# A fused attention and two-layer MLP kernel: its first stage in fixed instruction sequences, with three pairs' row sums made behind the values product

## The chip, the cores and the metric

One core of a Trainium2 chip runs the whole program. The metric is device time in microseconds, median of the runs; lower is better. The before kernel has 880.47 us.

## What is computed

The reference is windowed attention, its output laid out as 2304 tokens of 512 columns, then two MLP layers, all in f32:

```python
scores = scale * np.matmul(q, k.transpose(0, 1, 3, 2))      # 4 batches, 8 heads, 576 positions, 64 columns
mask = (rel >= 0) & (rel < 64)                              # rel = query position - key position
scores = np.where(mask, scores, -1000000000.0)
attn = np.exp(scores - np.max(scores, axis=-1, keepdims=True))
attn = attn / (np.sum(attn, axis=-1, keepdims=True) + 1e-09)
x = np.matmul(attn, v)                                      # then (2304, 512)
x = np.maximum(x @ w_in, 0.0) ** 2 @ w_out                  # 512 -> 2048 -> 512
x = (x @ w_a) * (x @ w_b) @ w_out2                          # 512 -> 1536 -> 512
```

## The kernel before

**Two stages.** In the first, attention runs together with the first six of sixteen blocks of 128 hidden columns of the first layer (`G1`). In the second (`paired`, from the first `ps_in` product at L1062 to the end) the other ten and the second layer run in a form that saves products. The change rewrites the first stage; the second keeps its code.

**Attention** goes by 18 pairs `c` of 64-query chunks (128 tokens). One pair is this chain of steps, each a key that the code names: loads `k`, `q`, `v`; `S` (scores of eight heads in two groups `j`, TensorE, L375); `M` (mask, scale and row minimum, DVE, L392); `E` (exponential with its row sums in an accumulator, ACT, L403); `N` (1 over the sum, times the probabilities, DVE, L410 to L417); `Tr` (transpose, TensorE, L437); `pT` (copy out of PSUM, ACT, L441); `V` (product with the values, which gives the output transposed, TensorE, L451); `xh`, `xl` (the output split in a high and a low half, ACT L460 and DVE L464).

**The first layer** goes by units `k`: one block of hidden columns for a block of tokens (`BLOCKS`; for the first 512 tokens in halves of 256). `H` is the projection, three products for each of four parts (high times high, high times low, low times high), `r` the relu, `g` and `hi` squares, `lo` the difference, `O` the product with `w_out` into four PSUM banks. In the first token block `H.k.0` and `O.k.0` are the two products that need only high halves. Weights are loaded as 64-bit floats (`ld`) and split on ACT and DVE (`high`, `low`, `sign`, `shift`, `sum`, then `whi`, `wlo`). After the last block `ev` and `st` move the sums to DRAM.

**What sets the order.** Every step is put in a `Plan` with its engine, an assumed cost, what it depends on and a rank; `Plan.issue` lays the steps out by a greedy list schedule and records the instructions in that order, and each engine then runs its own queue strictly in order. `PHASE` gives the ranks. In its first 45 us the plan also places fillers: where it expects TensorE to be free, `busy` (L419) records products with a bf16 identity that nobody reads, at L431 into the next step's own bank, at L424 into an old one. The SP queue issues nearly all loads and stores; `k` of pair 0 goes on ACT's queue.

Of the kernel before, what the change touches and what calls it, by code (L numbers as in the profile page):

```python
# [38 lines left out]
    "i0 o0 p0 p1 i1 p2 o1 p3 a0 i2 a1 o2 p4 b2 a2 b0 p5 i3 o3 i4 a3 b1 f4 o4 b3 i5 f5 n n p6 p7 n n p8 p9 n n p10 "  # L39
    "n n p11 x0 p12 n n n p13 n n n p14 p15 x1 x2 n p16 o5 p17 n n n n n n n n n"  # L40
# [4 lines left out]
FORM = "vvaavaaavavvvavaaaaavvvvvvaaaaaavaaavavvavvvaaavvaaaaavavvvvvava"  # L45
LATER = 4
NPR = NCH // 2
# [12 lines left out]
class Plan:  # L60
# [10 lines left out]
    def add(self, key, eng, cost, fn, deps=(), rank=0.0, take=None, give=None, size=0.0, lag=0.0):  # L71
        assert key not in self.at, key
        self.at[key] = len(self.steps)
        self.steps.append((key, eng, cost, fn, [d for d in deps if d is not None], rank, take, give, size, lag))

    def fill(self, order, slots):
# [11 lines left out]
        for t, _, i in order:  # L88
            key, eng, cost = self.steps[i][:3]
            if eng == "PE" and t < FILL_END:  # L90
                if t - at > 0.45 and (key[0] in ("S", "Tr", "V") or key[0] == "H" and len(key) == 3):
# [6 lines left out]
    def issue(self):  # L98
# [19 lines left out]
        held_to = {}  # L118

# [3 lines left out]
        while len(order) < n:  # L123
            best = None
            for eng, c in cand.items():
                opts = []
                for i in c:
# [23 lines left out]
            cand[eng].remove(i)  # L151
            if eng == "PE":
                if of_run(key) and not in_run:
                    cost += 0.23
                in_run = of_run(key)
            free[eng] = t + cost
            end = t + cost + (0.22 if eng == "PE" else 0.16)
# [21 lines left out]
def kernel(  # L179
# [51 lines left out]
    zero_bf = mk_p.tile([P, 1], BF16, name="zero_bf")  # L231

    plan = Plan({"w": 4, "ev": 3, "pr": 5})
# [59 lines left out]

    def c_hi(i):
        hi = T["wh", seq[i]] = ring_w.tile([P, 512], F32R, tag=f"wh{i}", name="wh")
        T["wl", seq[i]] = ring_w.tile([P, 512], F32R, tag=f"wl{i}", name="wl")
        nc.scalar.copy(out=hi, in_=T["a", i])
# [6 lines left out]
    cv_done, s_done = [], []  # L304

    def conv_raw(key, rank):
# [9 lines left out]
        add(("high", i), "ACT", 0.58, f(c_high), [("ld", i), *cv_free], rank)  # L316
        add(("low", i), "ACT", 0.65, f(c_low), [("ld", i), *cv_free, s_free], rank)
        add(("sign", i), "DVE", 0.35, f(c_sign), [("ld", i), *cv_free, s_free], rank)
        add(("shift", i), "DVE", 0.34, f(c_shift), [("high", i)], rank)
        add(("sum", i), "DVE", 0.61, f(c_sum), [("shift", i), ("low", i), ("sign", i)], rank)  # L320
        return i

    def conv(key, rank):
        i = conv_raw(key, rank)
        f = lambda g: (lambda: g(i))
        add(("whi", i), "ACT", 0.52, f(c_hi), [("sum", i)], rank)
        add(("wlo", i), "DVE", 0.61, f(c_lo), [("whi", i)], rank)
# [79 lines left out]

    def a_plus(c, j):
# [3 lines left out]
    def a_norm(c, j):  # L412
# [4 lines left out]
        nc.vector.tensor_tensor(out=p, in0=p, in1=ri.unsqueeze(2).to_broadcast([P, NHP, P]), op=ALU.mult)  # L417

# [54 lines left out]
    last_h = {}  # L473
# [13 lines left out]
    def attention(c, rank):  # L487
        f = lambda g, *a: (lambda: g(c, *a))
# [8 lines left out]
        for j in range(2):  # L497
            ps = ("S", c) if c >= S_ACC and j else None
            add(("M", c, j), "DVE", 0.88, f(a_max, j), [("S", c), old("Tr", j), "masks"], rank, give=ps)
            pool = c >= ON_POOL  # L500
            add(("E", c, j), "ACT", 1.57, f(a_exp, j), [("M", c, j), old("Tr", j)], rank, lag=-0.6)
            if pool:
                add(("n", c, j), "POOL", 0.4, f(a_plus, j), [("E", c, j)], rank)
            add(("N", c, j), "DVE", 0.87 if pool else 1.02, f(a_norm, j), [("n" if pool else "E", c, j)], rank)
# [8 lines left out]
            add(("pT", c, j), "ACT", 0.49, f(a_copy, j), [("Tr", c, j), old("V")], rank, give=("Tr", c, j))  # L513
        after = [("Tr", c + 1, 0)] if JOIN <= c + 1 < NPR else []
        add(("V", c), "PE", 1.08 if run else 1.1, f(a_values), [("pT", c, 0), ("pT", c, 1), ("v", c), *after], rank, take="w")
        add(("xh", c), "ACT", 0.49, f(a_xh), [("V", c), *window_free(x_of[c][0])], rank)
        add(("xl", c), "DVE", 0.61, f(a_xl), [("xh", c)], rank, give=("V", c))
# [52 lines left out]
    def unit1(t, u, cols, rank):  # L570
        k = len(units)
        n = cols.stop - cols.start
# [930 lines left out]
```

## Time and profile before

| | us |
|---|---|
| median of 3 runs (lowest, highest) | 880.47 (879.64, 881.55) |
| span of the profiled execution | 878.4 |
| TensorE busy in it | 869.8 (99%) |
| DVE, ACT busy in it | 590.1 (67%), 490.1 (56%) |

The page gives the profiled execution by its span alone; no time of its own stands beside it. Busy time is modelled from pipelined products and counts the fillers, so 99% does not say that TensorE does useful work all the time: for that one reads its waits and the fillers' rows.

### The profile page before, as it was taken

What the parts mean: (1) busy time and instruction counts of PE and PEld (TensorE: products, weight loads), DVE (VectorE), ACT (ScalarE), POOL (GpSimd) and SP (SyncE); (2) the same over time, 40 slices, a digit from 0 to 9 for tenths busy, and PEclk for the clock granted to TensorE, in tenths of its full rate; (3) what the DMA queues carried; (4) which work ended last, traced back from release to release, by engine and by line L of the source; (5) the groups of instructions that cost most, each with busy time, mean ns of one, the idle gap of its engine ahead of it and who ended that gap; (6) DMA issues with size and microseconds to landing.
All of it is one profiled execution on the core that took longest, in us unless ns stands there. A gap on an engine that the chain in (4) does not pass through costs nothing.

```text
span 878.4 us, 15421 instructions
## 1 busy us (share of the span) xinstructions
PE 869.8 (99%) x5689; PEld 804.0 (92%) x5689; DVE 590.1 (67%) x1416; ACT 490.1 (56%) x1173; POOL 12.5 (1%) x49
## 2 busy tenths in 40 slices
PE   8999999999999999999999999999999999999998
PEld 4888988888999999999999999899999999999987
DVE  6999858668774777466878747776743687343424
ACT  7998867658773667356665554655522554221301
POOL 1000000000000000000000000000000000000000
PEclk9999999999999999999999999999999999999999
DMA  9996966747898637649596797424847352636331
GB/s 325 320 323 207 363 239 207 279 178 291 287 378 329 226 125 272 253 147 385 179 397 235 268 355 297 140 91 131 293 159 259 140 182 83 242 143 215 144 132 72
DMA packets 79562, 204.03 MB, mean 232 GB/s; under 512 B 7296, under 2 KB 33152, under 8 KB 79488
## 3 DMA queue, kind: packets, MB, share of 16 engines
q1 hardware_dynamic: 78816, 202.67, 64.4%
q8 instruction: 45, 0.74, 0.4%
q10 hardware_dynamic: 672, 0.39, 0.1%
q14 instruction: 29, 0.24, 0.1%
HBM read 146.41 MB, written 56.62 MB: 231 GB/s over the span
## 4 chain that ended last, share of the span: by engine, by line
PE 95%; DMA 2%; DVE 1%; ACT 1%; issue 0%; SPq 0%
PE acc L238 13%; PE acc L239 13%; PE acc L240 13%; PE ps_aX L1062 9%; PE ps_bX L1062 9%; PE ps_inX L1062 7%; PE ps_aZ L1062 4%; PE ps_bZ L1062 4%; PE ps_inZ L1062 4%; PE ps_in L238 2%; PE ps_in L239 2%; PE ps_in L240 2%; PE ps_bY L1062 2%; PE ps_aY L1062 2%; PE ps_inY L1062 2%; PE ps_s L375 2%
## 5 line engine op out<-in xcount | busy, mean ns | idle before, releaser
L1098 ACT COPY e<-ps_aX 128x384 f32<-128x384 f32 x36 | 17.3, 481 | 98.2 <-PE ps_aX L1062 96.6
L403 ACT ACTIVATE p<-p,nm 128x128 f32<-128x128 f32 x144 | 55.8, 391 | 7.5 <-DVE nm L392 7.5
L1062 PE MATMUL ps_inX<-xb,w 128*128 128x384 f32 x270 | 54.0, 334 | 0.0
L277 ACT ACTIVATE s<-raw 128x512 uint16<-128x512 uint32 x68 | 53.4, 786 | 0.0
L272 ACT ACTIVATE a<-raw 128x512 f32<-128x512 f32 x68 | 45.5, 669 | 13.1 <-DVE w L997 5.8
L292 DVE CUSTOM_DVE_ANT_0 a<-a,s 128x1024 uint16<-128x1024 uint16 x68 | 46.4, 688 | 7.5 <-ACT s L277 6.2
L1062 PEld LDWEIGHTS ps_inX<-xb,w 128*128 128x128 f32 x270 | 47.5, 188 | 0.0
L1062 PE MATMUL ps_bX<-xb,w 128*128 128x384 f32 x234 | 46.9, 334 | 0.0
L1062 PE MATMUL ps_aX<-xb,w 128*128 128x384 f32 x210 | 42.4, 336 | 0.0
L1062 PEld LDWEIGHTS ps_bX<-xb,w 128*128 128x128 f32 x234 | 41.3, 188 | 1.0
L1102 DVE TENSOR_TENSOR e<-e,ps_aY 128x384 f32<-128x384 f32 x18 | 10.0, 554 | 46.5 <-PE ps_aY L1062 42.5
L1314 DVE TENSOR_TENSOR pr<-acc,pr 128x512 f32<-128x512 f32 x33 | 22.5, 689 | 27.5 <-PE acc L240 15.3
L1062 PEld LDWEIGHTS ps_aX<-xb,w 128*128 128x128 f32 x210 | 37.1, 188 | 1.2
L729 DVE TENSOR_TENSOR hl<-bt,hl 128x768 fp32r<-128x768 f32 x33 | 31.4, 953 | 8.7 <-ACT hl L726 8.7
L240 PE MATMUL acc<-w,gh 128*128 128x512 f32 (+1 forms) x95 | 36.8, 387 | 0.0
L239 PE MATMUL acc<-w,gh 128*128 128x512 f32 (+1 forms) x95 | 36.7, 387 | 0.0
L238 PE MATMUL acc<-w,gh 128*128 128x512 f32 (+1 forms) x95 | 36.5, 384 | 0.0
L238 PE MATMUL acc<-eh,wh 128*128 128x512 f32 (+1 forms) x96 | 36.1, 376 | 0.0
L238 PE MATMUL ps_in<-win,wh 128*128 128x512 f32 (+1 forms) x96 | 35.5, 370 | 0.0
L239 PE MATMUL acc<-el,wh 128*128 128x512 f32 (+1 forms) x96 | 34.9, 363 | 0.0
L240 PE MATMUL acc<-eh,wl 128*128 128x512 f32 (+1 forms) x96 | 34.9, 363 | 0.0
L240 PE MATMUL ps_in<-win,wl 128*128 128x512 f32 (+1 forms) x96 | 34.8, 363 | 0.0
(238 smaller groups left out, 2517.1 us busy)
## 6 DMA issues: line engine op xcount, KB each, us to landing
xb<-xop SPq DMA_DIRECT2D x44, 768.0 KB, 9.2
x<-xop SPq DMA_DIRECT2D x35, 768.0 KB, 6.6
xop<-hl SPq DMA_DIRECT2D x33, 768.0 KB, 4.8
raw<-in_w_out_dram SPq DMA_DIRECT2D x28, 512.0 KB, 4.7
q_sb<-in_qbd_dram SPq DMA_DIRECT2D x18, 512.0 KB, 6.7
pr<-part SPq DMA_DIRECT2D x48, 192.0 KB, 4.4
part<-pr SPq DMA_DIRECT2D x36, 256.0 KB, 2.5
pr<-part SPq DMA_DIRECT2D x33, 256.0 KB, 3.5
```

Source lines behind the costliest of these rows:

```text
L238: nc.tensor.matmul(ps, ah, bh, start=first, stop=False)
L239: nc.tensor.matmul(ps, ah, bl, start=False, stop=False)
L240: nc.tensor.matmul(ps, al, bh, start=False, stop=last)
L272: nc.scalar.activation(out=cv_tiles(i)[0], in_=T["raw", i][:, :, 1].bitcast(F32), func=AF.Copy, scale=2.0 ** -112)
L277: nc.scalar.activation(out=cv_tiles(i)[1][:, :, 0], in_=T["raw", i][:, :, 0], func=AF.Copy, scale=2.0 ** -29)
L292: nc.vector.tensor_tensor(out=a, in0=a, in1=s, op=ALU.add)
L375: nc.tensor.matmul(T["s", c, j][e * W:(e + 1) * W, hp, :], T["q", c][r, e, hp, r], T["k", c][r, hp, e * W:e * W + P], start=True, stop=Tru ...
L403: nc.scalar.activation(out=T["p", c, j][:, hp, :], in_=T["p", c, j][:, hp, :], func=AF.Exp, bias=T["nm", c, j][:, hp:hp + 1], scale=-1.0, ...
L729: nc.vector.tensor_tensor(out=hl(n)[:, 1], in0=view(o), in1=hl(n)[:, 0].bitcast(F32), op=ALU.subtract)
L1062: nc.tensor.matmul(ps, w[:, a, cs], x[:, b, c], start=o < 3 and not c and not n, stop=c == 1 and n == 2, skip_group_check=True,)
L1098: nc.scalar.copy(out=c_tile(i), in_=T[copied[i][0], q])
L1314: nc.vector.tensor_tensor(out=ev, in0=T["acc2", ri, s, m][f.start // 256][:, f], in1=ev, op=ALU.add)
```

## The change

Five things change, all in the first stage.

1. `SEQUENCE` lists, for TensorE, DVE, ACT and SP, the keys of the first stage in a fixed order; `Plan.issue` takes from an engine's list first and falls back to the greedy choice when it is used up. Where a key stands in a list also says on which engine the step runs (`on`, `either`), so copies, relus and `whi` may go to DVE instead of ACT.
2. Pairs 0 to 2 (`DEFER`) skip `N`. Their exponentials have no accumulator; `V` is made with operands swapped (`a_rows`: tokens in rows), and beside it eight products of the unscaled probabilities with a column pair of ones give the row sums; `R` (`a_quotient`) multiplies the result by 1 over the sums; `Tx` (`a_turn`) transposes it by four products; then `xh`, `xl`.
3. `PHASE` names unit and token block, so blocks of hidden columns come in another order.
4. `hi` may be a copy of `g` on DVE (`cut`), `r` a maximum on DVE.
5. The assumed costs are new numbers; the fillers are placed by the same rule, also before `Tx`.

```diff
+SEQUENCE = {
+    "PE": (
+        "S.0 S.1 Tr.0.0 Tr.0.1 V.0 Tr.1.0 Tx.0 Tr.1.1 S.2 V.1 Tr.2.0 Tx.1 S.3 Tr.2.1 H.0.0 H.0 V.2 Tr.3.0 O.0.0 Tx.2 "
+        "S.4 H.1.0 H.1 Tr.3.1 S.5 V.3 H.2.0 O.0 H.2 O.1.0 H.3.0 Tr.4.0 Tr.4.1 H.3 O.1 H.4.0 S.6 V.4 H.4 O.2.0 H.5.0 "
+        "O.2 H.5 O.3.0 H.6.0 O.3 H.6 O.4.0 Tr.5.0 Tr.5.1 S.7 V.5 O.4 H.7.0 O.5.0 H.7 O.5 H.8.0 O.6.0 H.8 Tr.6.0 S.8 "
...
+DEFER = "111000000000"
...
+        named = {key if isinstance(key, str) else ".".join(map(str, key)): i for key, i in self.at.items()}
+        first_of = {eng: [named[w] for w in names.split()][::-1] for eng, names in SEQUENCE.items()}
...
+                if first_of.get(eng):
+                    c = [i for i in c if i == first_of[eng][-1]]
...
+    def a_exp_only(c, j):
...
+            nc.scalar.activation(
+                out=T["p", c, j][:, hp, :], in_=T["p", c, j][:, hp, :], func=AF.Exp,
+                bias=T["nm", c, j][:, hp:hp + 1], scale=-1.0,
+                accum_out=T["rd", c][:, hp, j:j + 1] if DEFER[c] == "2" else None,
+            )
...
+    def a_rows(c):
...
+                for e in range(2):
+                    r = slice(e * W, (e + 1) * W)
+                    nc.tensor.matmul(
+                        o[r, h * D:(h + 1) * D], T["pT", c, j][:, hp, r], T["v", c][:, e, h * D:(h + 1) * D],
+                        start=True, stop=True,
+                    )
+                if DEFER[c] == "1":
+                    nc.tensor.matmul(
+                        total[:, 2 * h:2 * h + 2], T["pT", c, j][:, hp, :], ones, start=True, stop=True,
+                    )
...
+    def a_quotient(c):
...
+        nc.vector.tensor_scalar(out=ri, in0=sums, scalar1=1e-9, scalar2=None, op0=ALU.add)
+        nc.vector.reciprocal(out=ri, in_=ri)
+        nc.vector.tensor_tensor(
+            out=T["p", c, 0].rearrange("p a (b d) -> p (a b) d", d=D),
+            in0=T["o", c].rearrange("p a (b d) -> p (a b) d", d=D),
+            in1=ri.unsqueeze(2).to_broadcast([P, 2 * NHP, D]), op=ALU.mult,
+        )
+
+    def a_turn(c):
...
+        for f in range(KC):
+            nc.tensor.transpose(ps[:, f, :], T["p", c, 0][:, f, :], ident)
...
+            if cut:
+                top(T["hi", k], T["g", k])
+            else:
+                nc.scalar.activation(out=T["hi", k], in_=T["r", k], func=AF.Square)
...
+        nc.gpsimd.memset(ones, 1.0)
```

Two places show how the instructions move. The first is the start of SP's queue, which issues the loads (`raw` is a weight load, `q_sb`, `k_sb`, `v_sb` the attention inputs). Before:

```order
L269 DMA raw_152<-in_w_in_dram 128x1024
L269 DMA raw_157<-in_w_out_dram 128x1024
L348 DMA q_sb_177<-in_qbd_dram 128x2x512
L344 DMA k_sb_179<-in_kT_dram 128x4x192
L348 DMA q_sb_181<-in_qbd_dram 128x2x512
L359 DMA v_sb_183<-in_vwin_dram 64x512
L360 DMA v_sb_183<-in_vwin_dram 64x512
L356 DMA v_sb_183<-in_vwin_dram 128x512
```

And in the changed program:

```order
L434 DMA q_sb_154<-in_qbd_dram 128x2x512
L434 DMA q_sb_159<-in_qbd_dram 128x2x512
L430 DMA k_sb_179<-in_kT_dram 128x4x192
L339 DMA raw_181<-in_w_in_dram 128x1024
L445 DMA v_sb_183<-in_vwin_dram 64x512
L446 DMA v_sb_183<-in_vwin_dram 64x512
L442 DMA v_sb_183<-in_vwin_dram 128x512
L339 DMA raw_187<-in_w_out_dram 128x1024
```

The two query loads and the keys of pair 1 now stand ahead of both weight loads. The second place is TensorE around the values of pair 0, with the transposes of pair 1 behind them (`ps_p` holds transposed probabilities, `ps_o` the values product, `ident_bf` marks a filler). Before:

```order
L437 MATMUL ps_p<-ident,p 128x128 x4
L431 LDWEIGHTS ident_bf
L431 MATMUL ps_o<-ident_bf 128x512
L431 LDWEIGHTS ident_bf
L431 MATMUL ps_o<-ident_bf 128x512
L431 LDWEIGHTS ident_bf
L431 MATMUL ps_o<-ident_bf 128x512
L451 MATMUL ps_o<-pT,v_sb 64x64 x16
L437 MATMUL ps_p<-ident,p 128x128 x4
```

In the changed program, from the last of the eight products with ones to the turn (L603, into `ps_x`):

```order
L581 MATMUL ps_p<-ones,pT 128x2
L543 MATMUL ps_p<-ident,p 128x128 x4
L537 LDWEIGHTS ident_bf
L537 MATMUL ps_x<-ident_bf 128x512
L537 LDWEIGHTS ident_bf
L537 MATMUL ps_x<-ident_bf 128x512
L537 LDWEIGHTS ident_bf
L537 MATMUL ps_x<-ident_bf 128x512
L537 LDWEIGHTS ident_bf
L537 MATMUL ps_x<-ident_bf 128x512
L603 MATMUL ps_x<-ident,p 128x128 x4
```

Products with ones stand between the values products, and the turn, a step of its own, stands behind the next pair's transposes with four fillers ahead of it. In all, TensorE's queue has 55 fillers before and 25 now: 7 before `S.0`, 4 before `S.1`, 4 before `V.0`, 4 before `Tx.0` and 6 before `Tr.2.0`.

## Rows read from the trace of the kernel before

**Rows 1.** The page: TensorE's busy time, and its granted clock by slice.
```profile
PE 869.8 (99%) x5689; PEld 804.0 (92%) x5689; DVE 590.1 (67%) x1416; ACT 490.1 (56%) x1173; POOL 12.5 (1%) x49
...
PEclk9999999999999999999999999999999999999999
```

**Rows 2.** Waits of PE, whole span: us in total, times, longest.
```profile
PE ps_s L375 <- DMA q_sb<-in_qbd_dram: 1.9, 2, 1.0
...
PE ps_p L437 <- DVE p L417: 1.2, 4, 0.5
```

**Rows 3.** Windows: stretch, length, PE, PEld, DVE, ACT, POOL, PEclk, DMA share, GB/s.
```profile
0.00:10.00 10.00, 7.38 (x54) 3.27 (x54) 4.09 (x8) 5.10 (x7) 3.24 (x19) 1.00 0.84 288
20.00:30.00 10.00, 10.00 (x141) 7.34 (x139) 9.65 (x48) 9.96 (x36) 0.63 (x1) 1.00 0.98 336
60.00:70.00 10.00, 10.00 (x59) 8.82 (x58) 9.86 (x27) 9.40 (x29) 0.44 (x2) 1.00 0.78 277
70.00:80.00 10.00, 10.00 (x121) 9.13 (x120) 9.81 (x31) 7.92 (x21) 0.00 (x0) 1.00 0.57 197
80.00:90.00 10.00, 10.00 (x126) 9.25 (x124) 8.71 (x32) 9.37 (x36) 1.31 (x3) 1.00 0.83 271
```

**Rows 4.** Timeline of PE: start us, us, line, names, count, idle before and its releaser.
```profile
1.70 5.58 PE L431 MATMUL ps_s<-ident_bf 128*128 128x512 bf16 x18 [1.70 <-POOL ident_bf L1381]
8.20 1.10 PE L375 MATMUL ps_s<-k_sb,q_sb 64*64 64x128 f32 x32 [0.92 <-DMA q_sb<-in_qbd_dram]
...
11.27 1.10 PE L375 MATMUL ps_s<-k_sb,q_sb 64*64 64x128 f32 x32 [1.00 <-DMA q_sb<-in_qbd_dram]
...
25.36 0.38 PE L542 MATMUL ps_in<-win,wh 128*128 128x256 f32 x1
...
223.80 1.23 PE L1062 MATMUL ps_inX<-x,w 128*128 128x384 f32 x6
```

**Rows 5.** Groups by line and form, PE, 0 to 60 us: fillers alone.
```profile
L431 PE MATMUL ps_s<-ident_bf 128*128 128x512 bf16 x22 | 6.6, 463 | 1.7 <-POOL ident_bf L1381 1.7
...
L424 PE MATMUL ps_s<-ident_bf 128*128 128x512 bf16 x16 | 3.8, 380 | 0.0
...
L431 PE MATMUL ps_p<-ident_bf 128*128 128x512 bf16 x14 | 3.5, 380 | 0.0
L431 PE MATMUL ps_o<-ident_bf 128*128 128x512 bf16 x3 | 0.8, 379 | 0.0
```

**Rows 6.** Timeline of PE, 75 us: products back to back.
```profile
75.01 0.28 PE L240 MATMUL ps_in<-win,wl 128*128 128x256 f32 x1
75.13 1.04 PE L437 MATMUL ps_p<-ident,p 128*128 128x128 f32 x8
76.10 1.10 PE L375 MATMUL ps_s<-k_sb,q_sb 64*64 64x128 f32 x32
77.13 1.15 PE L451 MATMUL ps_o<-pT,v_sb 128*64 128x64 f32 x32
```

**Rows 7.** Timeline of ACT and its queue, first 5 us.
```profile
0.73 0.64 ACTq L344 DMA_DIRECT2D k_sb<-in_kT_dram  x1
...
4.23 0.68 ACT L272 ACTIVATE a<-raw 128x512 f32<-128x512 f32 x1 [1.55 <-DMA raw<-in_w_in_dram]
```

**Rows 8.** DMA issues: count, KB each, median us from issue to landing.
```profile
q_sb<-in_qbd_dram SPq DMA_DIRECT2D x18, 512.0 KB, 6.7
...
k_sb<-in_kT_dram SPq DMA_DIRECT2D x17, 384.0 KB, 6.3
...
k_sb<-in_kT_dram ACTq DMA_DIRECT2D x1, 256.0 KB, 6.2
```

**Rows 9.** Groups by line and form, ACT, 0 to 60 us: busy us, mean ns.
```profile
L403 ACT ACTIVATION_READ_ACCUMULATOR p<-p,nm 128x1 f32 x48 | 9.1, 189 | 0.0
```

**Rows 10.** Groups by line and form, DVE, 0 to 60 us: busy us, mean ns.
```profile
L392 DVE CUSTOM_DVE_ANT_0 p<-ps_s,mask_sb 128x128 f32<-128x128 f32 x52 | 11.8, 285 | 0.5 <-PE ps_s L375 0.4
L417 DVE TENSOR_TENSOR p<-p,ri 128x512 f32<-128x512 f32 x12 | 8.3, 692 | 0.7
```

More of the change, by code (lines that the diff above doesn't have):

```diff
@@ L73, in add @@
         self.at[key] = len(self.steps)
-        self.steps.append((key, eng, cost, fn, [d for d in deps if d is not None], rank, take, give, size, lag))
+        deps = [d for d in deps if d is not None]
+        self.steps.append((key, eng, cost, fn, deps, rank, take, give, size, lag))
     def fill(self, order, slots):
@@ L156, in issue @@
             free[eng] = t + cost
-            end = t + cost + (0.22 if eng == "PE" else 0.16)
+            end = t + cost + (0.22 if eng == "PE" else 0.14)
             if size:
@@ L304, with dve, either @@
     cv_done, s_done = [], []
+    def dve(n):
+        return 0.065 + 0.00106 * n
+    def either(key, first, act, dve, *args, **kw):
+        eng = on(key, "DVE" if first == "V" else "ACT")
+        add(key, eng, act if eng == "ACT" else dve, *args, **kw)
+        ways[key] = act, dve
+    ways = plan.ways = {}
     def conv_raw(key, rank):
@@ L568, in back, with unit1 @@
         return [(x, k - 2) for x in names] if k >= 2 else []
-    def unit1(t, u, cols, rank):
+    def unit1(t, u, cols, fresh, last, run, rank):
         k = len(units)
         n = cols.stop - cols.start
+        assert t + 2 not in begun, "its window is taken"
         units.append((t, u))
-        first, last = u == G1[0], u == G1[-1]
-        width = BLOCKS[t][1]
         early = t == 0
@@ L579, in unit1 @@
         i, o = num["in", u], num["out", u]
[L580 to L581 removed]
+        square = on(("g", k), "ACT" if FORM[k % len(FORM)] in "an" else "DVE") == "ACT"
+        cut = on(("hi", k), "DVE" if FORM[k % len(FORM)] in "nm" else "ACT") == "DVE"
         def r_():
             T["r", k] = e_tile("r", k, n)
[L585 removed]
+            if on(("r", k), "ACT") == "DVE":
+                nc.vector.tensor_scalar(out=T["r", k], in0=T["H", k], scalar1=0.0, scalar2=None, op0=ALU.max)
+            else:
+                nc.scalar.activation(out=T["r", k], in_=T["H", k], func=AF.Relu)
         def g_():
@@ L808 @@
     UNIT = {0: 0, 1: 1, 2: 1, 3: 0}
-    def dve(n):
-        return 0.09 + n / 960
     def act(n):
@@ L1408, in nxt @@
         return rank[0]
-    halves = {"a": slice(0, 256), "b": slice(256, 512), "f": slice(0, 512)}
-    later = [(t, u) for t in range(1, len(BLOCKS)) for u in G1]
-    for w in PHASE.split():
-        what, x = w[0], int(w[1:] or 0)
-        if what == "n":
-            t, u = later.pop(0)
-            unit1(t, u, slice(0, BLOCKS[t][1]), nxt())
-        elif what == "x":
+    halves = {"a": slice(0, 256), "b": slice(256, 512)}
+    todo = PHASE.split()
+    runs, run_of = [], {}
+    for at, w in enumerate(todo):
+        if w[0].isdigit():
+            t = int(w[0])
+            if not runs or runs[-1][0] != t:
+                runs.append((t, []))
+            runs[-1][1].append(at)
+    for n, (t, members) in enumerate(runs):
+        before = sum(b == t for b, _ in runs[:n])
+        for at in members:
+            run_of[at] = at == members[0], at == members[-1], before
+    for at, w in enumerate(todo):
+        if w[0].isdigit():
+            t, u = int(w[0]), G1[int(w[2])]
+            unit1(t, u, halves.get(w[3:], slice(0, BLOCKS[t][1])), *run_of[at], nxt())
+            continue
+        what, x = w[0], int(w[1:])
+        if what == "x":
             prepare1(x, nxt())
```

153 lines of the change are left out of this document (104 added, 49 removed), and 49 rows, old and new, of tables (PHASE, SEQUENCE).

## The prediction

> **What bounds the kernel now.** The span says first where to look: TensorE is busy for 869.8 of 878.4 us, and its granted clock is full in every slice [rows 1]. Busy does not mean useful, so the waits come next. TensorE waits for others for 4.8 us in the whole span: 1.7 for its first weights [rows 4], 1.9 in two waits for a query load and 1.2 in four for the softmax [rows 2]. The timeline places the two loads at 8.20 and 11.27 us [rows 4]; the list has nothing else. From about 60 us on the kernel is a TensorE queue that never runs dry: a microsecond taken off before that point moves everything behind it.
>
> The windows show what the opening costs. DVE is busy 9.65 of 10 us in 20 to 30 and 9.86 in 60 to 70, ACT 9.96 in the former [rows 3]: the softmax and the weight splitting fill both, while TensorE, with little to do, runs fillers, products with the bf16 identity that nobody reads. They count as busy. Grouped by line, 55 fillers stand in the first 60 us [rows 5]; the first 18 take 5.58 us from 1.70 [rows 4], before the scores of pair 0 (S.0) start at 8.20. The other 37 cost 6.6 - 5.6 = 1.0, 3.5, 0.8 and 3.8, together 9.1 us [rows 4, 5], and the waits behind S.0 2.2 us (1.0 for the second query load, 1.2 for the softmax) [rows 2, 4]. So 8.2 us before S.0 and **11.3 us** after it are not work: 19.5 us is all that a better opening could give back.
>
> **The change part by part.** The sum has three terms.
>
> 1. **S.0 earlier.** S.0 needs q.0 and k.0. SP now issues q.0 first; before it stood third, behind two weight loads of 512 KB each. A 512 KB load in that first place had landed by 4.23 us, when ACT began on it [rows 7]; that is the lower bound. k.0 keeps its queue (ACT's) and its place, and landed 6.2 us after its issue at 0.73, that is at 6.9 [rows 7, 8]; that is the upper bound. I take **6.2**, nearer to k.0's own row, since it is the same transfer on the same queue and only its neighbours are lighter: 2.0 us less. The lower end would save little more, because S.1 comes next and needs q.1 and k.1: k.0, q.0, q.1 and k.1 are 256 + 512 + 512 + 384 = 1,664 KB, nearly the 1,792 KB (k.0, two weight loads, q.0) that stood before S.0 at 8.20. S.1 therefore starts near 8, whatever S.0 does, against 11.27 before.
>
> 2. **Fillers and waits after S.0.** The planner puts fillers where it expects TensorE to wait; the order of the changed program has 25 instead of 55, 7 before S.0 and 18 after it. I use their number only, not the planner's times. Before, 37 fillers stood for 11.3 us of gap, 0.305 each with the waits that came with them. 18 of them are **5.5 us**, 5.8 us less. If the waits go altogether and a filler costs what it does back to back (3.8/16 = 0.24 [rows 5]), it is 4.3; if the 2.2 us of waits stay in full beside 18 x 0.305, it is 7.7. I take the middle one, because the change thins out what fed both. Each exponential without its sum spares ACT a read of the accumulator, 189 ns long and partly overlapped [rows 9]: for the 24 of three pairs between 0 and 4.5 us. DVE gives up two multiplications of 128 by 512 per pair, 692 ns each [rows 10], for one as large, with the small steps ahead of it: some 2 us in all. None of that enters the sum by itself; it is what makes fewer fillers plausible, as both engines were full [rows 3].
>
> 3. **Work added on TensorE.** For each of three pairs, 8 products with ones and 4 turns. A turn is a transpose of 128 by 128, and 8 such take from 75.13 to 76.10, 0.121 each [rows 6]: 12 x 0.121 = 1.5. A product with ones loads 128 columns of weights and streams 2 columns; no row shows it. From below it is two of the values product's records (32 records in 1.15 us, 0.036 each, 64 columns of weights [rows 6]), 0.07; from above two transposes, 0.24. I take one transpose, 0.121, as its weights are as wide: 24 x 0.121 = 2.9 (1.6 to 5.8). Together **+4.4 us**. The values product itself only swaps its operands: 32 records as before.
>
> What I cost at nothing. The weight loads that step back on SP: weight 0 now has 1,664 KB before it, and its split into two halves used to begin at 4.23 [rows 7], while the first projection stood at 25.36 [rows 4]; of these 21 us it loses about five, the distance from 4.23 to the data of S.1 and its own transfer. The setting of the ones on POOL, two columns: the masks that it delays are wanted only behind S.0. The chain values, quotient, turn, copy is about 2 us longer per pair than values, copy; scores and transposes of the next pair stand between in TensorE's order, and what is not covered shows as the fillers already counted (4 before the first values product, 4 before the first turn, 6 before the first transposes of pair 2). The copies, relus and squares that change between ACT and DVE later: from 60 us on TensorE waited for neither [rows 2]. If that cover went, they would cost what the last rival says.
>
> Sum: -2.0 - 5.8 + 4.4 = **-3.4 us**, span 878.4 to 875.0. The profile gives no time of its own for that execution besides the span; the runs' median of 880.47 lies 2.1 above the span, which I carry over: **877.1 us**.
>
> Here a rule speaks against the change. The rows first: the 22 fillers of the first group last 463 ns on average, those at 22 to 29 us 380 [rows 5], all at a granted clock of 1.00 [rows 1]; 18 in 5.58 us are 1.3 us more than at 0.24, as if five or six had run at 1.2 GHz instead of 2.4. With 7 fillers instead of 18, TensorE falls idle at about 4.7 us, some 1.5 us before S.0. Against harm stands that S.1 took 1.10 us after 1.00 us of idle, as S.0 did [rows 4]. The Trainium skill, "TensorE: Matmul & The Clock Gate", Part 1, says that "the default state is throttled, and activity releases the throttle". By that rule S.0 could find the slow clock again, and the sum would be -1.5 instead of -3.4; by the row at 11.27 it stays as it is.
>
> **The rivals.**
>
> *The slow clock at S.0.* Then S.0 lasts 1.1 longer, and the four fillers queued before S.1 take twice 0.24: 1.0 more. They stand in order, so S.1 ends about 1.9 later than planned, and the softmax of pair 1 with it. -3.4 + 1.9 = -1.5: **879.0**. For it: fewer fillers, and the slow first ones. Against it: the row at 11.27.
>
> *The plan leaks.* The four short waits for the softmax (1.2 us [rows 2]) came on top of the fillers that were planned. A fixed order has no more slack than a planned one: in it one late load or one slow step holds all behind it on its queue. Six such waits of 0.4 beyond the counted ones give -3.4 + 2.4 = -1.0: **879.5**.
>
> *DVE becomes the bound: slower.* The scores of pair 7 now stand before the values of pair 5, with 7 projections and 4 output steps ahead; before, 12 and 9 stood ahead of them. Ten steps of at least 12 products, 0.12 us from one to the next [rows 6], are some 14 us of TensorE work that used to cover DVE; pair 9's values move ahead of 3 projections and 5 output steps. One pair asks DVE for two normalizations and a subtraction of 0.69 each and eight maxima of 11.8/52 = 0.23 [rows 10]: 3.9 us. In 60 to 90 DVE was free for only 0.1 + 0.2 + 1.3 = 1.6 us [rows 3]. If DVE is late for one and a half pairs, TensorE waits 6 us: -3.4 + 6 = +2.6, **883.1**. It decides from the point where these waits pass 3.4 us in all. Against it: DVE idles 5.9 us of the first 10 [rows 3] and starts on the softmax earlier now, and three pairs give 2 us back.
>
> *The change does not do what it says* is out: the changed order shows the exponentials without a sum, the ones and the turns.
>
> **How the numbers follow.** My forecast, the three terms within half the way to their ends (875.2 to 878.6), has 0.60; the slow clock 0.13, the leak 0.17, DVE as the bound 0.10. A measurement can tell about 0.2% from no change, 1.8 us: 878.7 and 882.2 are the borders. Faster takes the forecast and, since the slow clock lies just across the border, 0.04 of it and 0.02 of the leak: 0.66. Same: 0.09 + 0.15 + 0.02 = 0.26. Slower: 0.08. The range leaves out DVE as the bound and the corner in which all terms fall well (-4.0 - 7.0 + 3.1): 874.6 to 880.5.
>
> **What would show it.** S.0 near 6.2 and S.1 near 8 (before 8.20 and 11.27); one product with ones near 0.12 us; 18 fillers and waits of about 5.5 us in all between S.0 and 60 us; the first product of the paired stage at about 220.4 instead of 223.80 [rows 4]; from there to the end the same time as before. I am wrong if TensorE waits for DVE or for a load behind 60 us, if S.0 lasts 2 us, or if the paired stage, whose code only gets other weight slots, changes its length.

## The result, and the profile after

The change makes the kernel **slower**, by 1.0%: 889.63 us median (885.41 to 892.59, 4 runs) against 880.37 for the kernel before in the same comparison (879.64 to 881.55, 4 runs); ratio 1.0102, 95% interval 1.0085 to 1.012. A second set of runs gave 889.68 against 880.07 (1.0107, 1.0092 to 1.0122). 877.1 was predicted, with 880.5 as the upper end. One thing stands out before any trace is opened: the runs of the kernel before lie within 2 us, those of the change spread over 7, and their mean granted clocks are 0.996, 0.992 and 0.988.

The profiled execution took 885.41 us (span 883.6, clock 0.996), the fastest of them. Its page has TensorE as busy as before [rows 1], but one slice of the granted clock is no longer full:

```profile
PE 876.9 (99%) x5719; PEld 813.5 (92%) x5719; DVE 599.6 (68%) x1433; ACT 476.8 (54%) x1123; POOL 14.1 (2%) x50
...
PEclk8999999999999999999999999999999999999999
```

TensorE's waits of the whole span (us in total, times, longest) answer to [rows 2, 4]. The waits for the softmax are gone, those for loads have shrunk, and nothing is waited for behind 31.2 us:

```profile
PE ps_s L537 <- POOL ident_bf L1551: 1.7, 1, 1.7
PE ps_s L461 <- DMA k_sb<-in_kT_dram: 1.1, 2, 0.6
PE ps_in L705 <- DVE win L610: 0.2, 1, 0.2
PE ps_o L576 <- DMA v_sb<-in_vwin_dram: 0.2, 1, 0.2
```

So the loss is not waiting but work. The timeline of TensorE (start us, us, line, names, count, idle before) answers to [rows 4] and shows which; V.0 stands at 10.95 to 16.69, V.1 at 22.40 to 26.96:

```profile
1.71 3.10 PE L537 MATMUL ps_s<-ident_bf 128*128 128x512 bf16 x7 [1.71 <-POOL ident_bf L1551]
5.33 1.10 PE L461 MATMUL ps_s<-k_sb,q_sb 64*64 64x128 f32 x32 [0.53 <-DMA k_sb<-in_kT_dram]
6.37 1.04 PE L537 MATMUL ps_s<-ident_bf 128*128 128x512 bf16 x4
7.97 1.10 PE L461 MATMUL ps_s<-k_sb,q_sb 64*64 64x128 f32 x32 [0.57 <-DMA k_sb<-in_kT_dram]
...
9.94 1.03 PE L537 MATMUL ps_o<-ident_bf 128*128 128x512 bf16 x4
10.95 0.30 PE L576 MATMUL ps_o<-v_sb,pT 128*64 128x64 f32 x2
...
16.69 1.09 PE L543 MATMUL ps_p<-ident,p 128*128 128x128 f32 x4
17.58 1.91 PE L537 MATMUL ps_x<-ident_bf 128*128 128x512 bf16 x4
...
22.40 0.34 PE L576 MATMUL ps_o<-v_sb,pT 128*64 128x64 f32 x4
22.66 0.38 PE L581 MATMUL ps_p<-ones,pT 128*128 128x2 f32 x2
22.98 0.34 PE L576 MATMUL ps_o<-v_sb,pT 128*64 128x64 f32 x4
...
26.96 1.46 PE L530 MATMUL ps_s<-ident_bf 128*128 128x512 bf16 x6
...
31.14 0.39 PE L705 MATMUL ps_in<-win,wh 128*128 128x256 f32 x1 [0.23 <-DVE win L610]
...
229.31 1.23 PE L1232 MATMUL ps_inX<-x,w 128*128 128x384 f32 x6
```

S.0 and S.1 start as early as predicted. But V.1 lasts 26.96 - 22.40 = 4.56 us where the values product alone took about 1.1 [rows 6]: one head goes from 22.40 to 22.98, 0.26 us of values and 0.32 with the ones. The first projection, before at 25.36 [rows 4], stands at 31.14, the first product of the paired stage at 229.31 instead of 223.80: 5.5 us later. From there to the end it is 654.3 us as against 654.6 before. The lag is thus there by 31 us, 5.8 us, and hardly changes after it: V.2 takes 4.56 us as well (32.76 to 37.32), but the kernel before still has nine fillers and short waits in that stretch.

The granted clock has a part in it. Windows of 1 us (stretch, length, PE, PEld, DVE, ACT, POOL, PEclk, DMA share, GB/s):

```profile
13.00:14.00 1.00, 1.00 (x12) 0.84 (x12) 0.77 (x2) 1.00 (x5) 0.00 (x0) 1.00 1.08 368
14.00:15.00 1.00, 1.00 (x14) 0.89 (x12) 0.00 (x0) 1.00 (x4) 0.00 (x0) 0.92 1.10 395
15.00:16.00 1.00, 1.00 (x10) 0.87 (x10) 0.00 (x0) 0.53 (x1) 0.00 (x0) 0.50 1.04 391
...
21.00:22.00 1.00, 1.00 (x25) 0.87 (x28) 1.00 (x2) 0.59 (x1) 0.00 (x0) 0.67 1.04 387
22.00:23.00 1.00, 1.00 (x28) 0.74 (x19) 0.78 (x6) 0.09 (x1) 0.00 (x0) 1.00 0.37 135
```

The clock falls to half, from 2.4 to 1.2 GHz, within V.0 and stays there till some 21.7 us, though the profile has TensorE busy in all of each microsecond. The four fillers at 17.58 take 1.91 us, those at 9.94 1.03.

### The profile page after: what moved, and what is told of

The parts are those of the page before. It is cut to its first block, busy times and chain, and to the rows that moved or that the text cites. A ratio compares the mean times of both kernels' runs of the same rounds, so it can differ in the third digit from the quotient of the medians.

```text
span 883.6 us, 15433 instructions
## 1 busy us (share of the span) xinstructions
PE 876.9 (99%) x5719; PEld 813.5 (92%) x5719; DVE 599.6 (68%) x1433; ACT 476.8 (54%) x1123; POOL 14.1 (2%) x50
## 4 chain that ended last, share of the span: by engine, by line
PE 98%; DMA 1%; DVE 1%; SPq 0%; issue 0%; DVEq 0%
PE acc L308 13%; PE acc L309 12%; PE acc L310 12%; PE ps_aX L1232 9%; PE ps_bX L1232 8%; PE ps_inX L1232 7%; PE ps_aZ L1232 4%; PE ps_bZ L1232 4%; PE ps_inZ L1232 4%; PE ps_in L308 2%; PE ps_in L310 2%; PE ps_in L309 2%; PE ps_aY L1232 2%; PE ps_bY L1232 2%; PE ps_p L543 2%; PE ps_o L557 2%
## 5 line engine op out<-in xcount | busy, mean ns | idle before, releaser
L342 ACT ACTIVATE a<-raw 128x512 f32<-128x512 f32 x68 | 45.5, 669 | 19.0 <-DVE w L1144 10.4
L489 ACT ACTIVATE p<-p,nm 128x128 f32<-128x128 f32 x120 | 46.5, 391 | 7.5 <-DVE nm L478 7.5
L478 DVE CUSTOM_DVE_ANT_0 p<-ps_s,mask_sb 128x128 f32<-128x128 f32 x144 | 32.4, 284 | 9.0 <-PE ps_s L461 8.9
L1144 DVE TENSOR_TENSOR w<-a,w 128x256 fp32r<-128x256 f32 x79 | 31.4, 418 | 5.8 <-ACT w L1140 5.8
```

Of the source, the lines that this page charges most:

```text
L342: nc.scalar.activation(out=cv_tiles(i)[0], in_=T["raw", i][:, :, 1].bitcast(F32), func=AF.Copy, scale=2.0 ** -112)
L478: nc.vector.tensor_tensor_reduce(out=T["p", c, j][:, hp, :], in0=T["s", c, j][:, hp, :], in1=mask_sb[:, mask_of(c)], scale=-SCALE, scalar= ...
L489: nc.scalar.activation(out=T["p", c, j][:, hp, :], in_=T["p", c, j][:, hp, :], func=AF.Exp, bias=T["nm", c, j][:, hp:hp + 1], scale=-1.0, ...
L1144: nc.vector.tensor_tensor(out=w[:, 1], in0=at[o](), in1=w[:, 0].bitcast(F32), op=ALU.subtract)
```

## The experiments

Three theories were at hand: the products with ones are dear where they stand (A); thin products let the clock fall (B); the fixed order with the scaling behind the values product is slow in itself (C). All times are medians; each ratio is against the kernel before on the same chip.

### e1: the sums on ScalarE again

```diff
-                accum_out=T["rd", c][:, hp, j:j + 1] if DEFER[c] == "2" else None,
+                accum_out=T["rd", c][:, hp, j:j + 1],
...
-                if DEFER[c] == "1":
-                    nc.tensor.matmul(
-                        total[:, 2 * h:2 * h + 2], T["pT", c, j][:, hp, :], ones, start=True, stop=True,
-                    )
...
```

> The eight products with ones of each of the first three pairs are taken out; the row sums come again from ScalarE's accumulator, read out after each exp as in the kernel before. Order and fillers are those of the change. A, the products with ones are dear: in the changed kernel V.1 and V.2 take 4.56 us each where the values product before took 1.08, and V.0 some 6; without the ones three V of about 1.5 to 2.1 us remain, so some 8 to 10 us less on TensorE at the start, partly given back as waits for the exps (12 accumulator reads of 0.19 us more on ScalarE, 2.3 us): the first paired product at 221 to 224 instead of 229.3, the time 878 to 882. B, the clock alone (it fell to half from 15 to 21.6 us, about 3.3 us lost): without thin products no fall, 885.4 less 3.3, so 882 to 885, if the ones themselves cost next to nothing. C, the fixed order with the scaling behind the values product is slower by itself: 885 or more, the stretch stays long with TensorE waiting.

880.14 us, ratio 0.9995 (0.9986 to 1.0005), all clocks 0.998 or more. 9.5 us of the change's time go with the ones, by their price, by the clock or by both, and the paired stage starts at 223.06: C does not explain the loss. Nor is the scheme without the ones a gain, because TensorE now waits for the exps and what follows them (its waits, as above):

```profile
PE ps_p L543 <- DVE p L513: 1.6, 1, 1.6
PE ps_p L543 <- ACT pT L523: 1.2, 1, 1.2
...
PE ps_s L461 <- ACT pT L523: 0.8, 1, 0.8
...
```

### e2: the ones behind all values products of a pair

```diff
-                if DEFER[c] == "1":
-                    nc.tensor.matmul(
-                        total[:, 2 * h:2 * h + 2], T["pT", c, j][:, hp, :], ones, start=True, stop=True,
-                    )
+        for h in range(2 * NHP):
+            nc.tensor.matmul(
+                total[:, 2 * h:2 * h + 2], T["pT", c, h % 2][:, h // 2, :], ones, start=True, stop=True,
+            )
```

> All sixteen values products of a pair first, then its eight products with ones, in place of one product with ones behind each two values products. A1, the price comes of the alternation (weights of 64 and of 128 columns, two tiles of the array): V.1 and V.2 fall from 4.56 us to 3 or less and the time to 880 to 884. A2, the price is the product with ones itself (four passes with 128 columns of weights loaded for 2 columns moved): V.1 and V.2 stay at 4.2 to 4.6, the time 885 to 892. B, the clock: eight thin products stand in a row, so the clock falls at least as often as with the alternation; time 886 to 893, spread from run to run.

878.82 us, ratio 0.998 (0.997 to 0.9989): **faster than before** by 0.2%, with the same products as the change in another order. The timeline of TensorE:

```profile
1.70 3.17 PE L537 MATMUL ps_s<-ident_bf 128*128 128x512 bf16 x7 [1.70 <-POOL ident_bf L1552]
5.43 1.98 PE L461 MATMUL ps_s<-k_sb,q_sb 64*64 64x128 f32 x32 [0.56 <-DMA k_sb<-in_kT_dram]
7.34 1.89 PE L537 MATMUL ps_s<-ident_bf 128*128 128x512 bf16 x4
9.16 1.93 PE L461 MATMUL ps_s<-k_sb,q_sb 64*64 64x128 f32 x32
11.02 1.09 PE L543 MATMUL ps_p<-ident,p 128*128 128x128 f32 x8
...
19.29 1.15 PE L576 MATMUL ps_o<-v_sb,pT 128*64 128x64 f32 x32
20.37 1.95 PE L582 MATMUL ps_p<-ones,pT 128*128 128x2 f32 x16
22.17 1.46 PE L530 MATMUL ps_s<-ident_bf 128*128 128x512 bf16 x6
```

The values of a pair take 20.37 - 19.29 = 1.08 us, the eight products with ones 1.80: 0.225 each. V.1 falls from 4.56 to 2.88, so the alternation alone cost 1.68 us for a pair. That is A1. The eight products are 16 records of 0.112: each is done in two passes, each with its own 128 columns of weights. All ten runs have clock 1.00, so a row of eight thin products lets nothing fall.

This profile also shows S.0, the fillers and S.1 at half speed (1.98, 1.89, 1.93 us; 1.10, 1.04, 1.10 in the change's first profile). That is the prediction's rival of the slow clock, for which e5 was made. The durations tell it, not the windows, whose granted clock is 1.00 for 0 to 10 us.

### e3: two products with half the weights

```diff
-                        total[:, 2 * h:2 * h + 2], T["pT", c, j][:, hp, :], ones, start=True, stop=True,
+                        total[r, 2 * h:2 * h + 2], T["pT", c, j][:, hp, r], ones, start=True, stop=True,
```

(The statement now stands in the loop over `e`, behind each values product.)

> Each product with ones (128 columns of weights) becomes two of 64 columns with the same weights as the values product ahead of it: 16 in place of 8 for a pair. A1, the change between 64 and 128 columns is what costs: V falls to 3 us or less, time 879 to 884. A2, every thin product costs one load of its weights, whatever its width: 16 instead of 8, V.1 and V.2 rise to 6 us or more, time 888 to 896. B, the clock: more thin products, falls at least as often as in the change; 886 to 895.

878.49 us, 0.9981 (0.9972 to 0.9991), clock 0.999 or more. Twice as many products, yet V.1 takes 1.99 us in all:

```profile
19.11 0.34 PE L576 MATMUL ps_o<-v_sb,pT 128*64 128x64 f32 x4
19.28 0.24 PE L580 MATMUL ps_p<-ones,pT 128*64 128x2 f32 x4
19.37 0.33 PE L576 MATMUL ps_o<-v_sb,pT 128*64 128x64 f32 x4
...
21.10 1.47 PE L530 MATMUL ps_s<-ident_bf 128*128 128x512 bf16 x6
```

(1.99 - 1.08)/16 = 0.057 us for a product with the same 64 columns of weights as its neighbour (each record still has a load of its own); two of them do what one of 0.435 did in the change. A1 again; A2, by which every thin product costs the same, is out.

### e4: ones 64 columns wide

```diff
-    ones = mk_p.tile([P, 2], F32, name="ones")
+    ones = mk_p.tile([P, 64], F32, name="ones")
...
-                        total[:, 2 * h:2 * h + 2], T["pT", c, j][:, hp, :], ones, start=True, stop=True,
+                        total[:, 64 * h:64 * h + 64], T["pT", c, j][:, hp, :], ones, start=True, stop=True,
...
```

> The ones are 64 columns wide instead of 2, everything else is the change's. A, the price is the load of the weights: the extra 62 columns go under the load or add at most 4 x 62 columns at 2.4 GHz, 0.10 us, per product, 2.5 us in all; V.1 and V.2 4.6 to 5.4; if the clock has no part in it, 886 to 894, granted clock over the stretch as in the change. B, the clock falls because 2 columns leave the array empty: with 64 columns the granted clock stays at 1.00 from 14 to 22 us, V.0 takes about 5 us in place of 6 and nothing else runs at half speed: mean clock 0.998 or more in all runs, 881 to 885 with a small spread.

889.07 us, 1.0096 (1.008 to 1.0112), clocks 0.992 to 0.996. V.1 takes 28.00 - 22.93 = 5.07 us. At full clock a head takes 23.56 - 22.93 = 0.63 us, 0.05 more than in the change:

```profile
22.93 0.34 PE L576 MATMUL ps_o<-v_sb,pT 128*64 128x64 f32 x4
23.20 0.43 PE L581 MATMUL ps_p<-ones,pT 128*128 128x64 f32 x2
23.56 0.34 PE L576 MATMUL ps_o<-v_sb,pT 128*64 128x64 f32 x4
```

By the price of a filler, 0.24 us for 512 columns, the 62 columns more in two passes would take some 0.06, an estimate: they come on top here and do not go under the weights. The clock falls as with 2 columns, so B in the form "the product is too narrow" falls.

### e6: the ones two at a time

```diff
+            for j in range(2):
+                h = 2 * hp + j
+                nc.tensor.matmul(
+                    total[:, 2 * h:2 * h + 2], T["pT", c, j][:, hp, :], ones, start=True, stop=True,
+                )
```

(One level out, in the loop over `hp`, instead of behind each head.)

> The change with its products with ones put behind every four values products, two at a time: four changes from 64 to 128 columns of weights and back for a pair where the change has eight and the version with the ones last has one. A1, each change of width costs: V.1 took 4.56 us with eight and 1.08 + 1.80 = 2.88 with one, so (4.56 - 2.88)/7 = 0.24 us for each, and V.1 and V.2 now 2.88 + 3 x 0.24 = 3.6 us; the time from 878.8 + 3 x 3 x 0.24 = 881 up to 884 if the clock falls once. A2, it is not the changes but how far the ones stand from the values product that fills their wait: V.1 near 2.9 or near 4.5. On the clock: if the alternation is what lets it fall, the granted clock of the stretch lies under 1.00 in some runs here; if only a V of over 4 us does it, it stays at 1.00.

```profile
20.80 0.45 PE L576 MATMUL ps_o<-v_sb,pT 128*64 128x64 f32 x8
21.18 0.61 PE L582 MATMUL ps_p<-ones,pT 128*128 128x2 f32 x4
...
24.40 1.46 PE L530 MATMUL ps_s<-ident_bf 128*128 128x512 bf16 x6
```

V.1 takes 24.40 - 20.80 = 3.60 us, as worked out: with 8, 4 and 1 changes of width for a pair, 4.56, 3.60 and 2.88 us, **0.24 us for each change more** (7 times 0.24 is 1.68, 3 times 0.72). 883.33 us, 1.0035 (1.0021 to 1.0049). Its runs sort themselves by clock, but for one (882.46 at 1.000):

| mean clock of the run | time, us |
|---|---|
| 1.000 | 879.36, 882.46 |
| 0.996 | 882.04, 883.18, 883.18 |
| 0.994 | 883.47, 883.75, 884.47, 885.17 |
| 0.993 | 886.36 |

### e8 and e12: long rows of thin products without alternation

e8 is e2 with each product with ones done twice; e12 is e5 (below) with each of its products done three times.

```diff
-        for h in range(2 * NHP):
+        for h in [*range(2 * NHP)] * 2:
```

```diff
-                    nc.tensor.matmul(
-                        total[r, 2 * h:2 * h + 2], T["pT", c, j][:, hp, r], ones, start=True, stop=True,
-                    )
+                    for _ in range(3):
+                        nc.tensor.matmul(
+                            total[r, 2 * h:2 * h + 2], T["pT", c, j][:, hp, r], ones, start=True, stop=True,
+                        )
```

> The version with the ones last, each product with ones done twice (sixteen in a row, 3.6 us of them for each of the three pairs). On price: 8 x 0.225 = 1.80 us more for each pair, 5.4 in all, so 878.8 + 5.4 = 884.2 where TensorE never waits; less, 881 to 883, where the wait for the exps (which the version without products with ones showed as 3 to 5 us) takes it up. On the clock: if a long row of thin products lets it fall, the granted clock over the stretch falls below 1.00 and the mean clock of the runs to 0.996 or less, the time 885 or more; if it is the alternation of 64 and 128 columns, it stays at 1.00.

> The version with half weights and ten fillers, each product with ones done three times (48 of 64 columns of weights for a pair in place of 16). The price of one such product was (1.98 - 1.08)/16 = 0.056 us, so each V grows by 32 x 0.056 = 1.8 us to about 3.8, as long as that of the versions whose clock fell (3.6 to 5.2 us), while every product in it is four times cheaper than one with 128 columns of weights. If the length of a stretch of thin products is what lets the clock fall: V 3.8 us, mean clock 0.996 or less in most runs, 884 to 888. If it is the wait for weights of 128 columns: the clock stays at 1.00, 878.5 plus 3 x 1.8 less the waits of 1 to 3 us that it can cover, 881 to 884.

e8: 889.53 us, 1.0097 (1.0082 to 1.0112), clocks 0.992 to 0.994. e12: 886.65 us, 1.0073 (1.0056 to 1.009), clocks 0.996 and 0.997. The clock falls in both. In e8 no alternation is left and TensorE does not stand idle, so neither is needed for a fall. e12 has no weights of 128 columns in V, but it shows less: the fall of its profile stands in V.1, from 23.8 us, and just there TensorE stood idle for 1.08 us, till 23.98, for which the profile shows no cause; no other profile has that at a fall. V.0 before it, 11.59 to 16.04, kept the full clock, at 4.45 us where 3.8 was expected. In e8 the first fall comes near the end of the row of V.0:

```profile
13.73 4.09 PE L582 MATMUL ps_p<-ones,pT 128*128 128x2 f32 x32
17.67 1.09 PE L543 MATMUL ps_p<-ident,p 128*128 128x128 f32 x4
```

### e9: full products between the thin ones

```diff
+                if h in (1, 3, 5):
+                    for _ in range(2):
+                        nc.tensor.matmul(
+                            total[:, 256:], ident_bf, ident_bf.unsqueeze(1).to_broadcast([P, 2, P]), start=True,
+                            stop=True,
+                        )
```

> The change as it is, with two full products (128 columns of weights, 256 columns moved, into columns that nobody reads) behind every second head's product with ones: six for each V, 6 x 0.11 = 0.64 us. This takes the clock apart from the price. If the price of the alternation is 4.56 - 2.88 = 1.68 us for each V, and the rest of the change's loss is the clock, and full products between keep the clock up: every V takes 4.56 + 0.64 = 5.2 us, the clock is 1.00 in all runs, and the time is 878.8 + 3 x (5.2 - 2.88) = 885.8, with a spread of 2 us and not of 7: less than the change's 889.6 although more work is done. If the full products don't keep the clock: 890 to 895, clock 0.988 to 0.996. If the clock had no part in the loss: 889.6 + 1.9 = 891.5 at a clock of 1.00.

890.22 us, 1.0109 (1.0094 to 1.0124), clocks 0.990 to 0.994. The fillers did not keep the clock: the first expectation fell, the second came (V.1 28.32 - 23.04 = 5.28 us). The attempt to take clock and price apart in this way failed; e6's table and the next run come closer.

### e11: the change once more

No edit.

> The change once more, unchanged, on the same chip as the two others, for its spread: 885 to 893, and by the clock's share in the loss the time follows the mean clock of the run: about 885 to 886 at 0.996 and some 3 us more for each 0.004 less.

888.76, 888.84, 890.52 and 891.57 us at 0.992, 0.992, 0.988 and 0.988. The clock falls three times in the profiled run (span 887.0), in V.0, 0.4 us behind V.1 and in V.2; one window of 1 us out of each fall:

```profile
18.00:19.00 1.00, 1.00 (x4) 0.43 (x3) 0.94 (x2) 0.56 (x1) 0.00 (x0) 0.50 1.03 362
...
28.00:29.00 1.00, 1.00 (x5) 0.53 (x4) 1.00 (x3) 0.00 (x0) 0.00 (x0) 0.50 0.00 0
...
42.00:43.00 1.00, 1.00 (x15) 0.67 (x17) 0.00 (x0) 0.52 (x2) 0.00 (x0) 0.50 0.00 0
```

With the first four runs the change has 885.4 us at 0.996 (one run), 888.4 at 0.992 (mean of three) and 891.6 at 0.988 (mean of four): 3.1 us for each 0.004. Carried on to 1.000 that makes 882.3, an estimate of the change without falls. The windows bear it out: what the microseconds lack of the full clock adds up to 3.4 us in the change's first profile and to 6.8 in this one, and 883.6 - 3.4 and 887.0 - 6.8 are both 880.2 us of span, some 882.0 of time.

### e5 and e10: half weights, ten fillers ahead of S.0

```diff
-                busy(ps, plan.fills.get(("S", c)))
+                busy(ps, (0, 0, 10) if not c else plan.fills.get(("S", c)))
```

(On top of e3; e10 is the same kernel once more, with 11 runs.)

> The version with half weights (two products with ones of 64 columns of weights, behind the values product with the same weights; 878.5 us), with 10 fillers ahead of S.0 in place of 7. In its profile the fillers ended at 4.87, TensorE was idle for 0.97 us until k had landed, and S.0, the next fillers and most of S.1 ran at half speed (1.99, 1.89, 1.35 us; where S.0 began at full speed they took 1.10, 1.04, 1.10). D, the idle time ahead of S.0 is what leaves the engine slow: with it filled S.0 takes 1.10 us, S.1 ends near 9.1 to 9.6 instead of 10.87, and the time falls by 1.3 to 2 us: 876.5 to 877.2. E, how soon the engine becomes fast is a matter of when it began and not of the gap, or later waits (for the exps of the first pairs) take up what is won: S.0 at 2 us or S.1 early and the first H at the same time: 878 to 879.

> The version with half weights and ten fillers, once more, with more rounds, beside the change on the same chip. In its first profile the paired stage began 1.64 us sooner than with seven fillers (221.33 for 222.97), yet the end came 0.7 us later, with waits of TensorE for ScalarE (0.9 us) in the first products of the paired stage. If those waits belong to that one run: 877.0 to 877.8 in the median and no such wait in this profile. If they come with every early start: 878 to 878.5 and the waits are there again.

S.0 runs at full speed in both profiles and S.1 is over by 9.1; the paired stage starts at 221.33 and 221.24 us, 1.7 sooner than in e3 and 2.5 sooner than before. The gain is D's, but its reason is not: e12 has the same ten fillers and no idle time behind them, and its S.0 takes 1.39 us:

```profile
1.70 4.45 PE L537 MATMUL ps_s<-ident_bf 128*128 128x512 bf16 x10 [1.70 <-POOL ident_bf L1551]
6.08 1.39 PE L461 MATMUL ps_s<-k_sb,q_sb 64*64 64x128 f32 x32
```

The fillers ahead tell more than the idle time. Seven of them take 3.17 us in all seven profiles in which S.0 is slower than 1.10, and 3.04 to 3.14 in the three in which it is not, while the idle time is 0.47 to 1.14 us in the former and 0.53 to 0.86 in the latter. Ten take 3.72 and 4.12 in e5 and e10, and 4.45 in e12. So S.0 is fast where the last fillers already were: the engine had not become fast yet, as E says, rather than slow again. What sets that moment, which differs from run to run, is not shown.

In time e5 and e10 show nothing: 878.20 us, 0.9975 (0.9963 to 0.9986), and 878.81, 0.9984 (0.9975 to 0.9993), against e3's 878.49. What was won is given back behind: from the start of the paired stage it is 656.7 and 655.6 us instead of 654.3, and TensorE waits there for ScalarE, 0.9 us in e5 and 0.4 in e10, and 0.2 for a load in e5. The rest of the 1.3 to 2.4 us is not seen in any wait that the list shows. e6, whose paired stage starts as late as 228.28, has such a wait too (1.6 us; 656.2 us to the end), so the early start alone is not shown to be the cause. Timeline of e5 (S.0, the fillers, S.1, then the paired stage):

```profile
5.52 1.10 PE L461 MATMUL ps_s<-k_sb,q_sb 64*64 64x128 f32 x32
6.56 1.04 PE L537 MATMUL ps_s<-ident_bf 128*128 128x512 bf16 x4
8.09 1.10 PE L461 MATMUL ps_s<-k_sb,q_sb 64*64 64x128 f32 x32 [0.49 <-DMA k_sb<-in_kT_dram]
...
232.84 1.31 PE L1231 MATMUL ps_inX<-xb,w 128*128 128x384 f32 x6 [0.55 <-ACT e L1267]
```

### e7: the fixed order without the scaling behind

`DEFER` is all zeros, `Tx` and `R` leave the lists, and six `N` stand in VectorE's.

```diff
-DEFER = "111000000000"
+DEFER = "000000000000"
...
-        "M.0.0 M.0.1 M.1.0 sign.0 M.1.1 shift.0 sign.1 sum.0 R.0 shift.1 sum.1 whi.0 xl.0 wlo.0 M.2.0 M.2.1 R.1 wlo.1 "
+        "M.0.0 M.0.1 M.1.0 sign.0 M.1.1 N.0.0 N.0.1 shift.0 sign.1 sum.0 N.1.0 N.1.1 shift.1 sum.1 whi.0 xl.0 wlo.0 M.2.0 M.2.1 N.2.0 N.2.1 wlo.1 "
```

> The fixed order without the scaling behind the values product: no products with ones, no turns, the first three pairs' probabilities scaled by VectorE ahead of their transposes as in the kernel before (six such steps put back into VectorE's order behind their maxima), the rest of the order and of the loads as in the change. If what is won comes of the order and the earlier loads of the first pair alone: the same as the version with half weights, 877.5 to 879. If it comes of taking the scaling (0.98 us of VectorE each, and 0.6 us more on ScalarE for each exp with its sums) out of the chain from scores to values: the first values product stands some 3 us later, V.0 at 14 to 15 instead of 11 to 13, and the time is 880 to 883. The fixed order was made for the other scheme, so waits that it causes itself (more than 1 us for p or pT after 12 us) would make it slower still.

883.96 us, 1.005 (1.0029 to 1.007). S.0 and S.1 are as early as in the change, but V.0 begins at 14.37 and TensorE fills the time:

```profile
8.99 3.19 PE L537 MATMUL ps_p<-ident_bf 128*128 128x512 bf16 x14
...
15.76 2.55 PE L537 MATMUL ps_p<-ident_bf 128*128 128x512 bf16 x11
```

The paired stage starts at 226.80. The gain of the cheap versions thus comes of the scaling put behind, as e3 against e7 shows (878.49 and 883.96), not of the order or the loads alone; with the caveat that this order was written for the other scheme.

## Why the prediction was wrong, point by point

1. **S.0 earlier: right.** S.0 at 5.33 (6.2 taken, 4.23 and 6.9 the ends), S.1 at 7.97 ("near 8"). In the change's second profile, e11, S.0 starts at 5.61 but takes 1.98 us, and S.1 starts at 9.34: see 6.
2. **Fillers and waits after S.0: right, in part by luck.** The order has 18 fillers, as said; they take 1.04 + 1.03 + 1.91 + 1.46 = 5.4 us and the waits 0.57 + 0.19 + 0.23 = 1.0, together 6.4 where 5.5 stood (4.3 to 7.7); 0.9 of it is the one group at half the clock. Where V is short more waits come up: in e5 and e10 the 18 fillers take 4.6 us and the waits 2.9 and 2.3, together 7.4 and 6.9, near the upper end. The long V of the change covers them.
3. **Work added on TensorE: here it failed.** The turns were right: in e2, four of them from 17.16 to 17.65 us are 0.12 each. The step was: "I take one transpose, 0.121, as its weights are as wide". A product with ones cost (4.56 - 1.08)/8 = **0.435 us** where the change puts it, 3.6 times that and beyond the upper end of 0.24. Two errors are in it. The first was to be had from [rows 6]: 16 values products stand there as 32 records, so a product of this type takes two passes, each with its weights, and the upper end, two transposes, was the price (0.225 in e2). The second no row of before showed: 0.24 us for each further change between 64 and 128 columns of weights (e2, e6). 24 x 0.435 = 10.4 instead of 2.9, 7.5 more. Some of it covers the waits of 2: TensorE waits in e10 for p, v, win and eh 0.8 + 0.6 + 0.4 + 0.4 = 2.2 us, in the change for v and win 0.4. As an estimate, 7.5 - 1.8 = 5.7 leads from 877.1 to 882.8, beside the estimate of 882.3 of e11.
4. **The clock behind S.1: not foreseen.** From the estimate of 882.3 to the measured 889.7, 7.4 us, are the falls, one to three in a profiled run. The prediction had the clock as a question of idle time ahead of S.0 only. In the 54 runs of e1, e2, e3, e5, e7 and e10, whose V takes 1.1 to 2.9 us, the mean clock is 0.998 or more; of the 34 of the change, e4, e6, e8, e9 and e12, whose V takes 3.6 us and longer, 32 have 0.997 or less. That goes together; what makes the clock fall is not shown.
5. **What was costed at nothing: it held, but under cover.** No wait of TensorE behind 31.2 us, and the paired stage as long as before (654.3 and 654.6). Where V is short, TensorE does wait for the softmax (p, 0.8 us in e5 and e10), for the projection's input (win, 0.4) and at 52 us for ScalarE (eh, 0.6 and 0.4), and the paired stage grows in both.
6. **The rivals.** DVE as the bound did not come; slower came, by a mechanism that was not on the list, so its chance of 0.08 was tied to the wrong thing. In the change the plan did not leak; in e5 and e10 fillers and waits are 1.9 and 1.4 us above the 5.5 of the sum, most of that rival's 2.4. The slow clock at S.0 does come: of the ten profiles with seven fillers ahead of S.0, six have it at 1.98 or 1.99 us (e2, e3, e4, e6, e8, e11), three at 1.10 (the change's first, e1, e9), e7 at 1.24. The sign "S.0 lasts 2 us" was met. It was not the idle time, though, that the rival names: where S.0 is slow, the fillers ahead of it were slow to the last (e5). The row at 11.27 [rows 4], on which it was held unlikely, told nothing of an engine that had just begun. Its price, 1.9 us till the end of S.1, was near the upper end of what came (S.1 ends at 9.05 in e1, at 10.29 to 11.20 in the six), though e5 and e10 show no gain in time from its removal. On this the Trainium skill, "TensorE: Matmul & The Clock Gate", Part 1 ("the default state is throttled, and activity releases the throttle"), was the better guide.

With the products at the price that had been taken (48 of 0.057 = 2.7 us in e5 and e10, 2.9 predicted) the paired stage starts at 221.24 to 221.33 us, where 220.4 was predicted, and the times, 878.20 and 878.81, lie 1.1 and 1.7 us above 877.1. But for this term the sum would have come near, with waits that it had too small and a paired stage that grew.

The versions e2, e3, e5 and e10 beat both kernels, by 0.2% against the one before.

## What to carry to other kernels

Before a small product is added beside others, count its passes and look at the width of its weights: a product with its neighbour's weights cost 0.057 us here, one of another width 0.435. Keep products of one width together, and look for a long row of them in the granted clock and in the spread of the runs, not in the busy time, which says 1.00 throughout. Where a long step hides waits, a cheaper one will show them. A bound that rests on a record's price must ask how many records one statement makes.

## What the runs showed of the hardware that was not expected

- **A change of the weights' width costs.** From 64 to 128 columns and back, 0.24 us for each further place where products with ones stand beside values products (V of 4.56, 3.60, 2.88 us with 8, 4, 1 such places).
- **A thin product costs its weights.** With 128 columns of weights and 2 columns moved it took 0.112 us a pass (e2); 62 more columns moved added 0.05 us for a product of two passes (e4). The Trainium skill, "TensorE: Matmul & The Clock Gate", section "LDWEIGHTS (loading the stationary operand)", gives columns/1.2 ns for a load, 107 for 128 and 53 for 64, and the trace of e2 agrees: 0.112 us a pass with 128, and its load records last 192 ns on average with 128 columns and 138 with 64, 54 less. It is not the pace of a row: in e2 the 32 loads of the values products of a pair, 138 ns each, lie within 1.01 us and so overlap, at 1.08/32 = 34 ns a pass.
- **The clock can fall while TensorE is busy.** It fell to half from 14.8 to 21.7 us with TensorE busy in all of each microsecond, and one to three times in the profiles with such falls, for 64 columns moved as for 2 (e4), with full products between (e9) and without alternation (e8). The one fall without wide weights (e12) came with 1.08 us of idle time. What the chip counts is not settled by these runs.
- **A granted clock of 1.00 at the start is no sign of full speed.** In e2 the windows say 1.00 for 0 to 10 us, while S.0 takes 1.98 us and the fillers behind it 1.89, where 1.10 and 1.04 were seen at full speed.
